# Squares of the values: single steps for the first batch, places of `v32` for its loads, and no gate for the later batches

## The chip, the cores and the metric

The kernel runs on one core of one Trainium2 chip. A core has TensorE (PE, matmuls; PEld is its weight load), VectorE (DVE), ScalarE (ACT), GpSimd (POOL) and SyncE (SP), which here issues all transfers of data. Each engine works through its own queue in order. The metric is device microseconds per execution, 941.67 us before the change (median of 3 runs, 940.76 to 941.94).

## The reference

Attention with a local window (32 positions for heads 0 to 3, every fourth of 128 positions for heads 4 to 7) over 8 batches of 576 positions and 8 heads of 64, and behind it a layer norm, an up-projection to 2048 with ReLU, a down-projection to 512, and a residual:

```python
scores = scale * np.matmul(q, k.transpose(0, 1, 3, 2))
scores = np.where(masks, scores, -1e9)          # masks: window, or dilated window
attn = softmax(scores)                          # with 1e-09 in the denominator
x = np.matmul(attn, v)                          # heads side by side: (B, S, 512)
xn = (x - mean) / np.sqrt(var + 1e-06) * g_ln
out = x + np.maximum(xn @ w_ch1, 0.0) @ w_ch2
```

The two weights come as float64, all else as float32.

## The kernel before, in words

**Tiles.** The 4608 rows are 36 tiles (`NT`) of 128, nine (`TPP`) to two batches of the reference; three tiles (`NB`) make a block for the feed-forward part. A tile goes through these steps: L loads q, k and v; A splits them into pairs of float16; S computes the scores, M the softmax, V the product with the values, N the norm, T the transposes; U are its up-matmuls and D its down-matmuls, with the output at the end. From the third block on, U and D are taken together for a block (`b2.5` is the sixth step of block 2). Tiles 0 to 3 (`EARLY`) skip A and work on float32. The weights are converted by C (w1, loaded at L655) and W (w2, also L655), each load followed by an ACT operation (L659), three on DVE (L661, L662, L666) and matmuls (L673), and split into float16 pairs by s (w1) and P (w2) with ACT at L153 and DVE at L154. P0 needs the scale of all of w2. D needs P, and U needs s and T.

**The scale of the values.** A float16 split of v needs a power of two as a scale. `scale_v(t0, t1)` makes one for the tiles of a batch, of which there are four: tiles 3 to 8, 9 to 17, 18 to 26 and 27 to 35. For each tile it loads the values once more, 256 KB, into a place called `row` (L225), squares them on ACT with a sum over each row into a column of `v_sums` (L226), and then adds the columns on DVE (L228), adds over the partitions by a matmul on PE (L230), copies the result out (L232) and makes the scale with four small DVE operations (L132 to L142). The split of a tile's values (`prep_v`, in A) waits for that scale.

**Places.** A named place comes in a number of copies: `row` has two, shared by the masks (once, at the start), these loads, and the outputs y of the down-matmuls; `v32` has two, for the values of tiles from 3 on (L194, and L293 for tile 3); `v_sums` has one, so a batch can't square before the batch ahead of it has added its columns; `ps_v`, in PSUM, has one, shared by V of all tiles and by L230; `slot` has five, for weights being converted, early values, q and k of odd tiles, and the split halves.

**What sets the order.** All steps are registered by `unit(name, when, what, *after)` with a number `when`, made larger than that of each step it comes after; `MOVED` puts other numbers in place of some. The steps are then written out sorted by that number. The number is only an order: a scheduler takes the written program, with the earlier step as the more urgent, and for each engine picks, at each point of its own model of time, the most urgent instruction whose inputs and place are there. An instruction written late can so be placed ahead of one written early. The order that it settles on is fixed for the engines, which then wait on semaphores. `tc.issue_after(x)` adds the condition that what its block writes for the engine of `x` comes behind `x` in that engine's queue.

**Around the change.** The first batch's step is `v3`, at 66.0. A later batch is written by `scale_later(t)` at 2 behind the start of A of tile 5, 14 or 23, and its transfers are held in SP's queue behind the load of that tile's own values (`state["load", t]`). Tile 5's own load is in turn held behind the last weight load written before it (`after_weights`). For the second batch the number of the step is 112 + 2 = 114; the first outputs come after P7, over 124.2.

Of the kernel before, what the change touches and what calls it, by code (L numbers as in the profile page):

```python
# [10 lines left out]
F32 = mybir.dt.float32  # L11
I32 = mybir.dt.int32
AF = mybir.ActivationFunctionType
ALU = mybir.AluOpType
AX = mybir.AxisListType
PSUM = bass.MemoryType.PSUM

P = 128
H = 8
HP = 4  # L20
D = 64
DM = 512
# [7 lines left out]
TPP = 9  # L30
NB = 3
NQK = 2 * HP * P
NBLK = NT // NB
EARLY = 4
AHEAD = 64.3
GAP = 17.2
SOFTMAX, VALUES, READY = 0.9, 23.0, 21.7
LOAD = -12.6
PER_TILE = 21.7
CW, SLOTS = 2, 5  # L40
HG = 4
SUMS = 128
NW2 = 2
SIGN_BIT = -(2**31)
V_GROUPS = (EARLY - 1, TPP)

TIMES = {
    "C": (0.0, 12.0, 30.0, 40.0), "E": (2.0, 22.0, 50.0, 75.0), "W": (50.0, 3.2), "P": 104.0,
    "U": (42.0, 66.0, 84.0), "D": 106.0, "v": 70.0, "X": 84.0, "t": (88.0, 112.0),
}  # L50

MOVED = {
# [6 lines left out]
}  # L59
APART = 2  # L60

# [7 lines left out]
def attention_then_ffn(ctx: ExitStack, tc, qkv, masks, g, w1, w2, out):  # L69
    nc = tc.nc  # L70

    const = ctx.enter_context(tc.tile_pool(name="const", bufs=1))
    work = ctx.enter_context(tc.tile_pool(name="work", bufs=2))
# [53 lines left out]
    def pow2_of(bound, top, squared, name):  # L127

        at = 2.0**23
        e = (189 if squared else 253) + top  # L130
        k = work.tile([P, 2], I32, name="sc_k")
        nc.vector.tensor_scalar(  # L132
            k[:, 0:1], bound.bitcast(I32), scalar1=24 if squared else 23, scalar2=23,
            op0=ALU.logical_shift_right, op1=ALU.logical_shift_left,
        )
        nc.vector.tensor_scalar(
            k[:, 1:2], k[:, 0:1], scalar1=(e - 252) * at, scalar2=-1.0, op0=ALU.max, op1=ALU.mult
        )
        s = const.tile([P, 2], F32, name=name)
        si = s.bitcast(I32)  # L140
        nc.vector.tensor_scalar(si[:, 0:1], k[:, 1:2], scalar1=e * at, scalar2=None, op0=ALU.add)
        nc.vector.tensor_scalar(  # L142
            si[:, 1:2], k[:, 1:2], scalar1=-1.0, scalar2=(254 - e) * at, op0=ALU.mult, op1=ALU.add
        )
        return s
# [13 lines left out]
    state = {}  # L159
# [6 lines left out]
    def load_tile(t):  # L166
        with after_weights() if t < NB * 2 else nullcontext():
            load_tile_now(t)
# [28 lines left out]
    def load_ranges(t, v32):  # L197
# [17 lines left out]
                        )  # L215
        return x

    def scale_v(t0, t1):

        if t0 % TPP == 0 or t0 == EARLY - 1:  # L220
            state["v_sums"] = work.tile([P, TPP], F32, name="v_sums", bufs=1)
        sums = state["v_sums"]
        for t in range(t0, t1):
            vs = work.tile([P, DM], F32, name="row")
            nc.sync.dma_start(out=vs, in_=qkv[t, :, NQK:])  # L225
            nc.scalar.activation(vs, vs, AF.Square, accum_out=sums[:, t % TPP : t % TPP + 1])  # L226
        tot = work.tile([P, 1], F32, name="v_tot")
        nc.vector.reduce_sum(tot, sums[:, t0 % TPP : (t1 - 1) % TPP + 1], axis=AX.X)  # L228
        ps = ps_v.tile([P, 2, 512], F32, name="ps_v")[:, 0]
        nc.tensor.matmul(ps[:, 0:1], ones.broadcast_to([P, P]), tot, start=True, stop=True)  # L230
        ss = work.tile([P, 1], F32, name="v_ss")
        nc.vector.tensor_copy(ss, ps[:, 0:1])  # L232
        sv = pow2_of(ss, T_V, True, f"sv{t0}")
        for t in range(t0, t1):
            state["sv", t] = sv

    def scale_later(t):
        with tc.issue_after(state["load", t]):
            t0 = (t // TPP + 1) * TPP
            scale_v(t0, t0 + TPP)  # L240

    def stack_v(t):

# [500 lines left out]
    def unit(name, when, what, *after):  # L744

        when = MOVED.get(name, when)
        for a in after:
            if a in units:
                when = max(when, units[a][0] + 0.001)
        units[name] = (when, len(units), what)  # L750
        return when
# [4 lines left out]
    at, pace = TIMES["W"]  # L756
    for f in range(0, NFC, CW):
        unit(f"W{f}", at + pace * f / CW, lambda f=f: load_w2(f), f"W{f - CW}", f"s{f // 4}")
    for n in range(NFC // NW2):
        unit(f"P{n}", TIMES["P"] + 0.01 * n, lambda n=n: split_w2(n), f"W{NFC - CW}", f"P{n - 1}")  # L760
    for a, b in zip(V_GROUPS, V_GROUPS[1:]):
        unit(f"v{a}", TIMES["v"], lambda a=a, b=b: scale_v(a, b), f"V{a - 1}")

    start = TIMES["D"] + 10.4 * NB
    t_at = 0.0
    for b in range(NBLK):
        blk = dict(t0=b * NB, b=b)
        for i in range(NB):
            t = b * NB + i
            if t < EARLY:  # L770
                t_at = TIMES["E"][t]
                if t:
                    unit(f"L{t}", t_at - 8.0, lambda t=t: load_tile(t), f"V{t - 2}")
                else:
                    unit("L0", 0.5, load_first)
                for n, (name, what) in enumerate((
                    ("S", scores_early), ("M", softmax_early), ("V", values_early), ("N", norm),
                )):
                    unit(f"{name}{t}", t_at + 3.0 * n, lambda t=t, what=what: what(t), f"L{t}", f"{name}{t - 1}")
                unit(  # L780
                    f"T{t}", t_at + 10.0, lambda t=t, i=i, blk=blk: transposes(t, blk, i), f"N{t}",
                    f"P{NFC // NW2 - 1}" if b else None,
                )
                if t == EARLY - 1:
                    unit(f"A{t}", TIMES["X"], lambda t=t: split_last(t), f"v{t}", f"N{t}")
                continue
            if t - EARLY < len(TIMES["t"]):
                t_at = TIMES["t"][t - EARLY]
            else:
                t_at = max(t_at + GAP, start - AHEAD - PER_TILE * (NB - 1 - i))  # L790

            def do(name, when, what, *after):
                return unit(f"{name}{t}", t_at + when, lambda t=t: what(t), f"{name}{t - 1}", *after)

            unit(f"L{t}", units[f"A{t - 1}"][0] + LOAD, lambda t=t: load_tile(t), f"A{t - 2}")


            t_at = do("A", 0, attn_prep, f"L{t}", f"V{t - 2}")
            if t % TPP == 5 and t + 4 < NT:
                do("v", 2, scale_later, f"A{t}")  # L800
            do("S", 6, attn_scores, f"A{t}")
            do("M", SOFTMAX, attn_softmax, f"S{t}", f"V{t - 1}")
            do("V", VALUES, attn_values, f"M{t}")
            do("N", VALUES + 2, norm, f"V{t}")
            unit(
                f"T{t}", t_at + READY, lambda t=t, i=i, blk=blk: transposes(t, blk, i),
                f"N{t}", f"P{NFC // NW2 - 1}" if b else None, f"b{b - 2}",
            )
        ups, downs = ffn(blk, b < APART)
        if b < APART:  # L810
            for i in range(NB):
                t = b * NB + i
                when = TIMES["U"][t] if t < len(TIMES["U"]) else start
                for fq in range(NKC):
                    us = ups[(4 * i + fq) * 4 // HG : (4 * i + fq + 1) * 4 // HG]
                    when = unit(
                        f"U{t}.{fq}", when, lambda us=us: [what() for _, what in us],
                        f"T{t}", f"s{fq}", f"U{t}.{fq - 1}", f"U{t - 1}.{fq}", f"D{t - 1 - i}.{fq}",
                    )
                    when += sum(took for took, _ in us)  # L820
                if b == 0:
                    when = TIMES["D"] + 10.4 * i
                for p in range(NKC):
                    took, what = downs[4 * i + p]
                    when = unit(
                        f"D{t}.{p}", when, what,
                        f"P{(4 * p + 3) // NW2}", f"U{t}.{p}", f"D{t}.{p - 1}", f"D{t - 2}.3" if p == 0 else None,
                    )
                    when += took
                start = max(start, when) if b else start  # L830
            last = tuple(f"D{t}.{NKC - 1}" for t in range((b + 1) * NB))
            units[f"b{b}"] = (max(units[a][0] for a in last), len(units), lambda: None)
        else:
            when = max(start, units[f"T{b * NB + NB - 1}"][0] + 0.1, max(units[a][0] for a in last))
            for n, (took, what) in enumerate(ups + downs):
                name = f"b{b}" if n == len(ups) + len(downs) - 1 else f"b{b}.{n}"
                when = unit(name, when, what, f"T{b * NB + NB - 1}", f"b{b}.{n - 1}", *last) + took
            last = (f"b{b}",)
            start = max(start + PER_TILE * NB, when)
    for _, _, what in sorted(units.values(), key=lambda e: e[:2]):  # L840
# [72 lines left out]
```

## Time and profile before

| | |
|---|---|
| median of three runs | 941.67 us |
| profiled execution | 944.02 us |
| span of its instructions | 942.2 us |
| PE busy | 890.7 us, 95% |
| DVE busy | 634.2 us, 67% |
| ACT busy | 312.7 us, 33% |
| POOL busy | 312.3 us, 33% |
| loads of values for squares | 33 of 256 KB, first at 19.2 us, last at 543.6 us |
| squares on ACT | 33, first at 27.0 us, last at 546.5 us |
| mean granted PE clock | 0.985 |

Times in the views are microseconds from the start of the span. A row of the order of time gives the start, the length, the engine, the source line, the operation with the places it writes and reads, and in brackets how long its engine was idle before it and what ended that. PE is near full from about 140 us to the end; before that the weights are loaded and converted while the first tiles are worked on.

### The profile page before, as it was taken

The page shows a single profiled execution, that of the slowest core. Times are in us where ns is not written, and L with a number is a line of the kernel's source. Part 1 is how long each engine was busy: PE and PEld are TensorE (multiplying, and loading weights), DVE is VectorE, ACT ScalarE, POOL GpSimd, SP SyncE. Part 2 cuts the span into 40 slices and gives each one's busy share as a digit, 9 for nine tenths or more (in the row PEclk, how much of TensorE's full clock was granted, in tenths as well). Part 3 has the DMA queues.
Part 4 walks back from the last instruction along what each step waited for, and adds up shares of the span by engine and source line. Part 5 has one row for each costly group of instructions (what it writes and reads, how often), then busy time and mean ns, then how long its engine had stood idle before and what let it go on. Part 6 is the DMA issues. An engine that isn't in the chain of part 4 may idle for free.

```text
span 942.2 us, 18610 instructions
## 1 busy us (share of the span) xinstructions
PE 890.7 (95%) x7608; PEld 552.2 (59%) x7608; DVE 634.2 (67%) x1379; ACT 312.7 (33%) x588; POOL 312.3 (33%) x319
## 2 busy tenths in 40 slices
PE   4479789999999999999999999999999999999998
PEld 4379466777665555565565565565565565564553
DVE  4799658896977577786686686686686685660210
ACT  4556742334323343251241451241241341130110
POOL 1010273646234235454253353354243341120000
PEclk9979899999999999999999999999999999999999
DMA  7887872754344516446143654364043411010000
GB/s 241 311 229 229 187 176 50 153 122 115 66 75 93 148 52 133 92 71 136 37 80 71 169 105 71 89 123 90 30 88 69 87 27 37 21 24 23 12 1 34
DMA packets 79622, 93.39 MB, mean 99 GB/s; under 512 B 47920, under 2 KB 53680, under 8 KB 79536
## 3 DMA queue, kind: packets, MB, share of 16 engines
q1 hardware_dynamic: 79536, 92.21, 42.3%
q8 instruction: 59, 0.97, 0.4%
q14 instruction: 27, 0.22, 0.1%
HBM read 71.86 MB, written 9.44 MB: 86 GB/s over the span
## 4 chain that ended last, share of the span: by engine, by line
PE 81%; DMA 10%; ACT 3%; DVE 3%; issue 2%; SPq 1%; POOL 1%; ACTq 0%; DVEq 0%; POOLq 0%
PE ps_f L597 36%; PE ps_f L620 35%; PE ps_s L330 4%; PE ps_v L528 4%; DMA row<-in_qkv 4%; DMA slot<-in_w 3%; DMA xT<-xl 1%; ACT row L226 1%; DMA slot<-in_qkv 1%; DMA v<-in_qkv 0%; PE ps_f L673 0%; ACT w_sb L153 0%; DVE slot L662 0%; POOL slot L280 0%; DVE slot L154 0%
## 5 line engine op out<-in xcount | busy, mean ns | idle before, releaser
L620 PE MATMUL ps_f<-w_sb,hh 128*128 128x512 f16 x1152 | 345.0, 380 | 5.8 <-ACT w_sb L153 5.0
L597 PEld LDWEIGHTS <-w_sb 128*128 128x128 f16 x3072 | 256.0, 99 | 126.6 <-issue 4.6
L620 PE MATMUL ps_f<-w_sb,hl 128*128 128x512 f16 x576 | 219.1, 380 | 0.0
L597 PE MATMUL ps_f<-xT,w_sb 128*128 128x384 f16 (+1 forms) x1536 | 199.2, 289 | 2.9 <-DMA xT<-xh 2.4
L597 PE MATMUL ps_f<-w_sb 128*128 128x384 f16 (+1 forms) x1536 | 196.7, 287 | 0.0
L620 PEld LDWEIGHTS <-hh 128*128 128x128 f16 x1152 | 111.8, 98 | 131.5 <-issue 6.8
L603 ACT ACTIVATE hh<-ps_f 128x384 f16<-128x384 f32 (+1 forms) x184 | 91.1, 500 | 216.8 <-PE ps_f L597 216.8
L604 DVE SCALAR_TENSOR_TENSOR hl<-ps_f,hh 128x384 f16<-128x384 f32 (+1 forms) x184 | 100.2, 569 | 42.4 <-ACT hh L603 40.3
L620 PEld LDWEIGHTS <-hl 128*128 128x128 f16 x576 | 56.5, 98 | 67.1 <-issue 1.8
L362 DVE TENSOR_TENSOR sc<-ps_s,mask 32x256 f32<-32x256 f32 x128 | 53.6, 419 | 51.2 <-PE ps_s L330 49.8
L435 DVE STREAM_TRANSPOSE pt_d<-pk 32x256 f32<-32x256 f32 x128 | 79.4, 621 | 1.8
L626 DVE SCALAR_TENSOR_TENSOR row<-ps_f,s,x 128x512 f32<-128x512 f32 x36 | 27.0, 749 | 74.5 <-PE ps_f L620 74.0
L446 POOL TENSOR_TENSOR sc<-sc,mx 128x512 f32<-128x512 f32 x32 | 33.4, 1043 | 116.3 <-DVE mx L444 116.3
L451 ACT ACTIVATE p<-sc 128x512 f32<-128x512 f32 x32 | 20.2, 631 | 128.2 <-POOL sc L446 128.2
L569 POOL TENSOR_TENSOR xl<-xn,xh 128x512 f16<-128x512 f32 x36 | 42.0, 1166 | 59.1 <-ACT xh L568 49.8
L330 PE MATMUL ps_s<-slot 128*128 128x128 f16 (+1 forms) x768 | 58.8, 226 | 2.1 <-DVE sc L348 2.1
L330 PEld LDWEIGHTS <-slot 128*128 128x128 f16 x768 | 50.9, 99 | 12.7 <-DVE sc L348 3.0
L287 POOL COPY slot<-slot 128x128 f16<-128x128 f16 x56 | 17.5, 340 | 119.4 <-PE ps_v L528 119.3
L348 DVE TENSOR_TENSOR sc<-ps_s,mask 32x256 f32<-32x256 f32 x128 | 53.5, 418 | 4.9 <-PE ps_s L330 3.4
L453 POOL TENSOR_TENSOR pk<-p,pk 128x512 f16<-128x512 f32 x32 | 40.7, 1271 | 45.8 <-ACT pk L452 45.8
L458 DVE STREAM_TRANSPOSE pt_b<-pk 32x128 f16<-32x128 f16 x87 | 26.1, 300 | 42.0 <-ACT pk L452 28.4
L554 POOL TENSOR_TENSOR rstd<-rstd,mhalf 128x1 f32<-128x1 f32 x36 | 21.1, 587 | 94.9 <-DVE rstd L553 85.2
(100 smaller groups left out, 961.3 us busy)
## 6 DMA issues: line engine op xcount, KB each, us to landing
qk<-in_qkv SPq DMA_DIRECT2D x36, 512.0 KB, 6.9
slot<-in_qkv SPq DMA_DIRECT2D x32, 512.0 KB, 6.7
slot<-in_w SPq DMA_DIRECT2D x14, 1024.0 KB, 6.3
out_x<-row SPq DMA_DIRECT2D x36, 256.0 KB, 2.0
row<-in_qkv SPq DMA_DIRECT2D x33, 256.0 KB, 2.9
v<-in_qkv SPq DMA_DIRECT2D x33, 256.0 KB, 3.0
slot<-in_w SPq DMA_DIRECT2D x4, 512.0 KB, 7.3
slot<-in_qkv SPq DMA_DIRECT2D x28, 64.0 KB, 4.5
```

What stands on the lines that cost most here:

```text
L330: nc.tensor.matmul(out, lhs, rhs, start=(n == 0), stop=(n == len(terms) - 1))
L348: nc.vector.tensor_tensor(out=sc[pj, 0:HP, :], in0=ps[pj, :, W * j : W * j + 2 * W], in1=mask_16[pj, m : m + 1, :].broadcast_to([W, HP, 2 ...
L362: nc.vector.tensor_tensor(out=sc[pj, HP:H, :].rearrange("p h (t i) -> p h t i", t=2), in0=ps[pj].rearrange("p h (t c) -> p h t c", t=2)[:, ...
L435: nc.vector.transpose(dd[pj].rearrange("p t h (i r) -> p r t h i", r=DIL)[:, j], pk[pj, HP:H, :].rearrange("p h (t i) -> p t h i", t=2),)
L446: nc.gpsimd.tensor_tensor(out=sm, in0=sc, in1=mx.broadcast_to([P, H, 2 * W]), op=ALU.subtract)
L453: nc.gpsimd.tensor_tensor(out=pk16[:, :, :, 1], in0=p32, in1=pk16[:, :, :, 0], op=ALU.subtract)
L528: nc.tensor.matmul(oo, l, r, start=(n == 0), stop=(n == len(mm) - 1))
L569: nc.gpsimd.tensor_tensor(out=xl, in0=xn, in1=xh, op=ALU.subtract)
L597: nc.tensor.matmul(z[:, n], l, r, start=(m == 0), stop=(m == len(mm) - 1))
L603: nc.scalar.activation(hh, z, AF.Relu)
L604: nc.vector.scalar_tensor_tensor(out=hl, in0=z, scalar=0.0, in1=hh, op0=ALU.max, op1=ALU.subtract)
L620: nc.tensor.matmul(o, l, r, start=(f == 0 and m == 0), stop=(f == NFC - 1 and m == 2))
```

## The change

The first batch's step is taken apart. Each of its six tiles gets a load step `y3` to `y8` and a square step `z3` to `z8`: loads at 33, 38, 43, 48, 53 and 58, the square 6 behind its load; the rest (`v3`: sum, matmul, scale) follows at 33 + 5 × 6 + 6 = 69, and `v3` has left `MOVED`. The loads go to places of `v32`. The later batches stay one step each with loads in `row`, but the step now stands 10 (`LATER`) behind the start of A and not 2, after A of its tile and after `v3`, and the condition that held its transfers behind a load is gone.

```diff
+SQUARE = 6.0
+LATER = 10.0
...
-    "U": (42.0, 66.0, 84.0), "D": 106.0, "v": 70.0, "X": 84.0, "t": (88.0, 112.0),
+    "U": (42.0, 66.0, 84.0), "D": 106.0, "v": (33.0, 5.0), "X": 84.0, "t": (88.0, 112.0),
...
-    "W6": 65.8, "b2.5": 240.4, "b2.6": 228.4, "v3": 66.0,
+    "W6": 65.8, "b2.5": 240.4, "b2.6": 228.4,
...
+    def load_values(t, name):
+        state["vs", t] = work.tile([P, H, D], F32, name="v32") if name == "v32" else work.tile([P, DM], F32, name="row")
+        x = state["vs", t]
+        x = x.rearrange("p h d -> p (h d)") if name == "v32" else x
+        nc.sync.dma_start(out=x, in_=qkv[t, :, NQK:])
+        state["vs", t] = x
+
+    def square_values(t):
+        if t % TPP == 0 or t == EARLY - 1:
+            state["v_sums"] = work.tile([P, TPP], F32, name="v_sums", bufs=1)
+        vs = state.pop(("vs", t))
+        nc.scalar.activation(vs, vs, AF.Square, accum_out=state["v_sums"][:, t % TPP : t % TPP + 1])
+
     def scale_v(t0, t1):
 
-        if t0 % TPP == 0 or t0 == EARLY - 1:
-            state["v_sums"] = work.tile([P, TPP], F32, name="v_sums", bufs=1)
-        sums = state["v_sums"]
-        for t in range(t0, t1):
-            vs = work.tile([P, DM], F32, name="row")
-            nc.sync.dma_start(out=vs, in_=qkv[t, :, NQK:])
-            nc.scalar.activation(vs, vs, AF.Square, accum_out=sums[:, t % TPP : t % TPP + 1])
         tot = work.tile([P, 1], F32, name="v_tot")
-        nc.vector.reduce_sum(tot, sums[:, t0 % TPP : (t1 - 1) % TPP + 1], axis=AX.X)
+        nc.vector.reduce_sum(tot, state["v_sums"][:, t0 % TPP : (t1 - 1) % TPP + 1], axis=AX.X)
...
-    def scale_later(t):
-        with tc.issue_after(state["load", t]):
-            t0 = (t // TPP + 1) * TPP
-            scale_v(t0, t0 + TPP)
...
-    for a, b in zip(V_GROUPS, V_GROUPS[1:]):
-        unit(f"v{a}", TIMES["v"], lambda a=a, b=b: scale_v(a, b), f"V{a - 1}")
+    def unit_v(a, b, at, pace, name):
+
+        for t in range(a, b):
+            when = at + pace * (t - a)
+            unit(f"y{t}", when, lambda t=t: load_values(t, name), f"y{t - 1}")
+            unit(f"z{t}", when + SQUARE, lambda t=t: square_values(t), f"y{t}", f"z{t - 1}", f"v{a - TPP}", f"v{EARLY - 1}" if a == TPP else None)
+        unit(f"v{a}", at + pace * (b - a) + SQUARE, lambda: scale_v(a, b), f"z{b - 1}")
+
+    unit_v(EARLY - 1, TPP, TIMES["v"][0], TIMES["v"][1], "v32")
...
             if t % TPP == 5 and t + 4 < NT:
-                do("v", 2, scale_later, f"A{t}")
+                def later(t):
+                    for n in range(t + 4, t + 4 + TPP):
+                        load_values(n, "row")
+                        square_values(n)
+                    scale_v(t + 4, t + 4 + TPP)
+
+                unit(f"v{t + 4}", t_at + LATER, lambda t=t: later(t), f"A{t}", f"v{EARLY - 1}")
```

More of the change, by code (lines that the diff above doesn't have):

```diff
@@ L44 @@
 SIGN_BIT = -(2**31)
-V_GROUPS = (EARLY - 1, TPP)
 TIMES = {
     "C": (0.0, 12.0, 30.0, 40.0), "E": (2.0, 22.0, 50.0, 75.0), "W": (50.0, 3.2), "P": 104.0,
-    "U": (42.0, 66.0, 84.0), "D": 106.0, "v": 70.0, "X": 84.0, "t": (88.0, 112.0),
+    "U": (42.0, 66.0, 84.0), "D": 106.0, "v": (33.0, 5.0), "X": 84.0, "t": (88.0, 112.0),
 }
```

## The prediction

> **What bounds the kernel now.** I read the busy times first, then the windows, to see where TensorE (PE) isn't full.
>
> ```profile
> PE 890.7 (95%) x7608; PEld 552.2 (59%) x7608; DVE 634.2 (67%) x1379; ACT 312.7 (33%) x588; POOL 312.3 (33%) x319
> ```
> ```profile
> 20.00:40.00 20.00, 9.30 (x159) 8.06 (x159) 14.08 (x23) 9.00 (x16) 0.12 (x1) 1.00 0.97 360
> 40.00:60.00 20.00, 11.76 (x110) 10.54 (x110) 17.84 (x34) 14.19 (x31) 3.51 (x3) 0.77 0.90 240
> 60.00:80.00 20.00, 19.23 (x345) 18.48 (x344) 19.99 (x35) 10.46 (x14) 2.16 (x2) 0.89 0.87 225
> 80.00:100.00 20.00, 18.84 (x382) 18.17 (x380) 17.68 (x39) 12.90 (x31) 1.71 (x2) 1.00 0.53 190
> 100.00:120.00 20.00, 15.39 (x66) 7.09 (x66) 10.88 (x11) 16.19 (x34) 7.23 (x5) 0.83 0.94 201
> 120.00:140.00 20.00, 15.39 (x208) 13.00 (x206) 10.01 (x27) 10.11 (x22) 13.40 (x15) 0.91 0.72 168
> 320.00:340.00 20.00, 17.41 (x113) 10.37 (x112) 8.49 (x24) 9.93 (x26) 2.31 (x2) 0.93 0.40 119
> 500.00:560.00 60.00, 60.00 (x459) 34.90 (x458) 44.15 (x105) 23.65 (x50) 21.76 (x23) 1.00 0.50 112
> ```
>
> Each window lists its length, then the busy us of PE, weight loads, DVE, ACT and POOL, then PE's granted clock, the DMA share and GB/s. PE is idle 942.2 − 890.7 = 51.5 us, 30.1 of them in 20:140, and 2.59 in 320:340. Around the third batch of squares (500:560) it is full. Up to 140 us the limit changes: 20:40 is DMA (share 0.97), 60:80 is DVE (19.99 of 20), 100:120 is ACT (16.19) and DMA (0.94). So the change is worth what it does before 140 us, and a little in 320:340.
>
> Next, SyncE's queue (start, length, transfer):
>
> ```profile
> 17.69 1.51 SPq L655 DMA_DIRECT2D slot<-in_w  x2
> 19.24 1.17 SPq L225 DMA_DIRECT2D row<-in_qkv  x2
> 20.57 0.43 SPq L655 DMA_DIRECT2D slot<-in_w  x1
> 27.71 0.94 SPq L225 DMA_DIRECT2D row<-in_qkv  x2
> 28.74 0.90 SPq L655 DMA_DIRECT2D slot<-in_w  x2
> 31.62 1.71 SPq L225 DMA_DIRECT2D row<-in_qkv  x2
> 95.91 0.73 SPq L194 DMA_DIRECT2D v<-in_qkv  x1
> 96.70 0.89 SPq L225 DMA_DIRECT2D row<-in_qkv  x2
> 123.44 0.33 SPq L225 DMA_DIRECT2D row<-in_qkv  x1
> 242.80 0.36 SPq L634 DMA_DIRECT2D out_x<-row  x1
> 261.46 0.58 SPq L194 DMA_DIRECT2D v<-in_qkv  x1
> 289.94 0.55 SPq L634 DMA_DIRECT2D out_x<-row  x1
> 313.21 0.66 SPq L225 DMA_DIRECT2D row<-in_qkv  x1
> ```
>
> Two things are to be seen. First, the written order doesn't hold a transfer back when its place is free: the first batch's six loads stand at 66.0 (`MOVED["v3"]`), behind W4 at 48.5, yet leave from 19.24. The nine loads of the second batch leave right behind the load of tile 5's values (95.91 to 96.70): their gate held them. Second, places of one name go in written order: between the output at 242.80 and the one at 289.94 no load of the third batch took a `row`, though its gate, the load of tile 14, had passed at 261.46, by count of the values' loads.
>
> **The change part by part.** *No work is added.* 33 loads of 256 KB, 33 squares and four sums stay. A square has this price, with 0.187 for reading the sum:
>
> ```profile
> L226 ACT ACTIVATE row<-row x33: 615/630/693, 27.0 to 546.5; 128x512 f32<-128x512 f32 x33
> SPq L225 <- ACT row L226: 15.7, 10, 6.6
> ```
>
> So only times move. The second line is SyncE before 140 us: 15 loads, 15.7 us of it waiting for a square to give back a place, 1.05 us a load.
>
> *Batch 0 (tiles 3 to 8): two places in `v32` in place of two in `row`, each load and square a step of its own at 33 to 64.* As deep as before; `v32` isn't wanted until tile 4's load, after 80 us. The loads already ran at 19 to 33, ahead of the new positions, so I cost it at 0. The bounds: SyncE stands still from 21.00 to 27.71 behind the third load, 6.7 us; if the weights (28.74) now pass it, up to 6.7 us come back, and if the earlier positions put a load ahead of a weight's, 256 KB at the 360 GB/s of 20:40 is 0.73 us each, 4.4 us for six. This batch's sum and scale move from 66 to 69, off the path: 0.
>
> *Batch 1 (tiles 9 to 17): the gate goes, and both `row` places are empty but for the masks.* This is what matters. By the queue's first lesson the loads leave as soon as SyncE has nothing better, from about 21 us. The first two squares wait for `v_sums` until batch 0's sum has read it (45.75 below), the other seven loads for a square each. So 9 × 256 KB and 9 × 0.82 us of ACT (630 + 187 ns, 7.4 us in all) go from 96 to 131 into 21 to 96. What they did where they were:
>
> ```profile
> 45.75 0.15 DVE L228 TENSOR_REDUCE v_tot<-v_sums 128x1 f32<-128x6 f32 x1
> 98.64 0.58 DVE L727 TENSOR_SCALAR s<-s,s 128x1 f32<-128x1 f32 x4
> 98.96 0.72 ACT L153 ACTIVATE vh<-v,sv 128x512 f16<-128x512 f32 x1 [3.63 <-DMA v<-in_qkv]
> 99.59 0.63 ACT L226 ACTIVATE row<-row 128x512 f32<-128x512 f32 x1
> 102.06 0.63 ACT L226 ACTIVATE row<-row 128x512 f32<-128x512 f32 x1 [1.74 <-DMA row<-in_qkv]
> 102.69 2.17 ACT L153 ACTIVATE w_sb<-w_sb,s 128x1024 f16<-128x1024 f32 x2
> 103.87 0.59 PE L620 MATMUL ps_f<-w_sb,hh 128*128 128x512 f16 x1 [5.04 <-ACT w_sb L153]
> 123.36 2.61 PE L476 MATMUL ps_v<-slot,pt_d 64*128 64x65 f32 x32
> 131.10 0.16 DVE L228 TENSOR_REDUCE v_tot<-v_sums 128x1 f32<-128x9 f32 x1 [4.37 <-ACT row L226]
> 131.61 0.76 DVE L486 TENSOR_TENSOR x<-ps_v,rs 128x256 f32<-128x256 f32 x2
> 132.51 0.54 PE L230 MATMUL ps_v<-v_tot,ones 128*128 128x1 f32 x2 [4.61 <-DVE x L486]
> ```
>
> (a) PE waits 5.04 us for the first split of w2. Its scale is ready at 99.22 (98.64 + 0.58), and ACT is behind the vh at about 99.6, but two squares, the second waiting for its load, hold the split until 102.69. Without them it starts 3.1 us sooner: **−3.1**. The vh's wait for `v` stays, so not all 5.04 come back.
>
> (b) From 126.7 DVE stands behind the sum of batch 1, which waits 4.37 us for the last square (loaded at 123.44). Behind it in DVE's order is tile 3's x, whose PSUM place PE's L230 waits for, with all of PE's work behind it: 4.61 us. With the squares done early, x follows its matmuls (over at 126.0) at once: **−4.6**. What is late next is the ordinary queue of up-matmuls behind L230; PE is full from 132.5.
>
> (c) What the loads cost where they go. Two in 20:40 at 360 GB/s take 2 × 0.262 MB / 360 = 1.5 us from the weights. DMA idles there only 3%, so I count it whole. The seven gated ones: DMA's idle shares in 40 to 96 come to 2.0 + 2.6 + 7.5 = 12.1 us (0.10, 0.13 of 20 and 0.47 of 16), and 1.84 MB at 360 GB/s want 5.1 us. So bandwidth is there, but each can hold SyncE for 1.05 us with a weight load or a transpose behind it: 7 × 1.05 = 7.4 us. DVE, the limit in 60:80, has weights queued up, so I take a little over a quarter of that, 2.0. Together **+3.5**. Bounds: 0 (all in gaps) and 1.5 + 5.1 + 7.4 = 14.0 us (nothing hidden).
>
> On this the Trainium skill speaks against the change: "DMA: Bandwidth & Descriptors", section on the anatomy of one DMA, says that a semaphore wait is held at the issuing sequencer, ahead of dispatch, so that a transfer that waits for a square stops everything behind it. The trace agrees, with SyncE silent from 21.00 to 27.71; by it alone the 7.4 us would count whole and the sum would come to +1.2, which is rival B at work, with its price below.
>
> (d) The granted clock after both PE gaps:
>
> ```profile
> 103.87:109.00 5.13, 4.39 (x11) 1.51 (x11) 4.43 (x5) 5.13 (x9) 0.53 (x1) 0.53 0.95 232
> 132.50:137.00 4.50, 4.49 (x49) 4.33 (x50) 4.16 (x15) 0.55 (x2) 4.42 (x4) 0.62 0.06 15
> ```
>
> 5.13 × 0.47 = 2.4 us and 4.50 × 0.38 = 1.7 us are lost to it. A gap elsewhere would bring it back, so the sum takes 0 and the range up to −4.1. "TensorE: Matmul & The Clock Gate", Part 1, in the Trainium skill, gives a window of about 3.4 us of idling before the clock halves; by it the shortened first gap (5.04 − 3.1 = 1.9 us) and the closed second one would keep it, and the sum would be −8.3 us, which still lies in the forecast's own range. The trace shows only that gaps of 5.04 and 4.61 us drop it.
>
> *Batches 2 and 3: gate gone, ten instead of two behind the tile's start.* Their loads wait for the outputs ahead of them in the ring of `row`, not for the gate. I take 0; bounds −2.6 (the idle in 320:340) and +2.6 (as much again).
>
> **Sum**: −3.1 − 4.6 + 3.5 = −4.2 us. The profiled execution took 944.02 us, its span 942.2 and 1.8 around it; that would be 939.8. Against the median of three runs, 941.67, it is 937.5.
>
> **The rivals.** *B, the weights starve (slower).* Place: SyncE's and ACT's queues from 45 to 96, where the gap-filling loads and squares stand ahead of weights. Its price is (c) at its upper end, 14.0, less the 7.7 of (a) and (b): +6.3, about 948. It decides once the split of w2 is put off by over 7.7 us. For it: SyncE's 15.7 us of such waits, DVE full in 60:80. Against: the 12.1 us of DMA idling, and ACT idle 5.8 to 9.5 us in each window from 40 to 100.
>
> *C, the second batch doesn't move.* If SyncE or DVE's sum of batch 0 has no gap before the weights are through, the loads leave near 96 as before, and the sum with its stall at 131 stays: 941.7. For it: they now stand at 122, behind more work. Against: batch 0 went 47 units ahead of its position.
>
> *D, batch 0 helps too.* Its squares as early steps let weights pass SyncE's 6.7 us of standing: −10.9 us in all, about 931. For it, what the weights' conversion on ACT waited for, and the last weight's load:
>
> ```profile
> 38.79 1.12 ACT L659 ACTIVATE w_sb<-slot 128x1024 f32<-128x1024 f32 x1 [6.59 <-DMA slot<-in_w]
> L655 SPq DMA_DIRECT2D slot<-in_w x18: 368/390/942, 2.1 to 82.7; - x18
> ```
>
> The load of 28.74 came 6.59 us late for ACT. Against: two places as before, so the third load still needs a square.
>
> **How the numbers follow.** The forecast 0.42, B 0.33, C 0.15, D 0.10. The forecast's own range is 933 to 940. With (d) and 320:340 below D and (c) above, 930 to 949 holds the time 8 times in 10. A measurement tells 0.2%, 1.9 us, from no change: faster 0.42 + 0.10 = 0.52, same 0.15, slower 0.33.
>
> **What would show it.** Right: L225's loads of nine leave between 20 and 96, batch 1's last square ends before 96, the 4.37 and 4.61 us waits are gone, and PE's first down-matmul starts near 104.3 or sooner (103.87 − 3.1 + 3.5). Wrong: nine loads still behind 95.91 (C); or weight loads (L655) ending well after 82.7 us, where the last one issued, and the first down-matmul past 108 (B); or weights issued at 24 rather than 28.74 (D). An idle stretch of PE that grows after 140 us would be outside all of these.

## The result, and the profile after

The changed kernel takes 953.51 us (median of 4 runs, 950.83 to 955.03), against 941.81 us for the kernel before on the same chip: ratio 1.0119, interval 1.0090 to 1.0148, so slower by 11 us. The prediction said 937.5 us and faster.

The profiled execution's span is 952.4 us, up from 942.2 us. The page's busy times of the changed kernel:

```profile
PE 891.0 (94%) x7608; PEld 552.0 (58%) x7608; DVE 636.9 (67%) x1379; ACT 311.6 (33%) x588; POOL 313.0 (33%) x319
```

PE has the same work (890.7 before); its idle time grew from 51.5 to 61.4 us. The windows of the changed kernel (columns as in the prediction) say where:

```profile
40.00:60.00 20.00, 15.04 (x145) 14.08 (x146) 16.80 (x26) 15.09 (x32) 1.40 (x2) 0.66 0.87 269
60.00:80.00 20.00, 13.88 (x257) 12.57 (x255) 15.57 (x32) 10.30 (x19) 0.55 (x1) 0.76 0.87 276
80.00:100.00 20.00, 14.97 (x226) 14.01 (x224) 18.13 (x25) 12.84 (x32) 2.83 (x3) 0.98 0.49 164
100.00:120.00 20.00, 19.92 (x300) 14.06 (x305) 12.78 (x28) 13.80 (x28) 4.71 (x4) 1.00 0.65 142
120.00:140.00 20.00, 13.68 (x148) 9.43 (x142) 12.31 (x21) 9.26 (x15) 17.39 (x16) 0.91 0.65 146
340.00:360.00 20.00, 15.17 (x126) 9.28 (x125) 13.57 (x37) 8.60 (x20) 5.13 (x7) 1.00 0.55 93
```

And one window of the kernel before that the prediction doesn't show:

```profile
340.00:360.00 20.00, 20.00 (x195) 12.72 (x194) 17.38 (x44) 8.65 (x15) 11.67 (x12) 0.98 0.41 84
```

In 60:100 PE lost 9.2 us (28.85 busy, 38.07 before); 4.5 of that came back in 100:120, where 115 up-matmuls ran (none before), and 3.3 had been gained in 40:60 (15.04 busy). Then 120:140 lost 1.7, and the third batch's place, 340:360, lost 4.8. DVE, which was full in 60:80, had nothing to do for 4.4 us there: ACT, which converts the weights ahead of it, waited 7.5 us in this window for their loads (3.9 before), and DVE 3.4 for one of the conversions.

SyncE's queue of the changed kernel (start, length, transfer) shows that the second batch did move:

```profile
21.47 1.09 SPq L223 DMA_DIRECT2D row<-in_qkv  x2
...
63.66 1.56 SPq L223 DMA_DIRECT2D row<-in_qkv  x2
65.33 0.38 SPq L657 DMA_DIRECT2D slot<-in_w  x1
...
77.40 0.34 SPq L223 DMA_DIRECT2D row<-in_qkv  x1
...
87.33 0.38 SPq L657 DMA_DIRECT2D slot<-in_w  x1
```

Its nine loads leave from 21.47 to 77.40, and the last weight leaves at 87.33, not 82.7. The order of time in the changed kernel shows something that the prediction had not looked for:

```profile
92.46 2.61 PE L478 MATMUL ps_v<-slot,pt_d 64*128 64x65 f32 x32
98.84 0.35 PE L237 MATMUL ps_v<-v_tot,ones 128*128 128x1 f32 x2 [1.04 <-DVE x L488]
100.69 0.15 DVE L239 COPY v_ss<-ps_v 128x1 f32<-128x1 f32 x1
102.18 1.33 ACT L154 ACTIVATE vh<-v,sv 128x512 f16<-128x512 f32 x2
106.29 2.19 ACT L154 ACTIVATE w_sb<-w_sb,s 128x1024 f16<-128x1024 f32 x2 [2.30 <-DVE s L729]
107.77 0.59 PE L622 MATMUL ps_f<-w_sb,hh 128*128 128x512 f16 x2
```

The first batch's scale: its matmul L237 waits for tile 2's `x` and stands behind tile 2's product with the values (L478). In the kernel before it stood ahead of that product by 13 us:

```profile
77.46 0.30 PE L230 MATMUL ps_v<-v_tot,ones 128*128 128x1 f32 x2
90.52 2.61 PE L476 MATMUL ps_v<-slot,pt_d 64*128 64x65 f32 x32
91.01 0.71 ACT L153 ACTIVATE vh<-v,sv 128x512 f16<-128x512 f32 x1
```

So the first split of values (vh) went from 91.01 to 102.18 us.

### The profile page after: what moved, and what is told of

The parts are those of the page before. It is cut to its first block, busy times and chain, and to the rows that moved or that the text cites. A ratio compares the mean times of both kernels' runs of the same rounds, so it can differ in the third digit from the quotient of the medians.

```text
span 952.4 us, 18606 instructions
## 1 busy us (share of the span) xinstructions
PE 891.0 (94%) x7608; PEld 552.0 (58%) x7608; DVE 636.9 (67%) x1379; ACT 311.6 (33%) x588; POOL 313.0 (33%) x319
## 4 chain that ended last, share of the span: by engine, by line
PE 76%; DMA 4%; DVE 3%; POOL 3%; ACT 2%; issue 1%; SPq 1%; ACTq 0%; POOLq 0%; DVEq 0%
PE ps_f L622 35%; PE ps_f L599 33%; PE ps_s L332 4%; PE ps_v L530 4%; DMA qk<-in_qkv 1%; DMA row<-in_qkv 1%; POOL slot L282 1%; DVE pt_d L437 1%; POOL slot L311 1%; DMA xT<-xl 1%; DMA v<-in_qkv 1%; SPq L187 0%; POOL sc L448 0%; DVE pt_a L434 0%; DVE sc L364 0%
```

## The experiments

The change was taken apart into four: the single steps with `v32`, the place of `v3` in the written order (66 or 69), the gate, and the position of the later batches (2 or 10). These are most of their combinations; the time of each is a median, its ratio is to the kernel before on the same chip.

| kernel | steps, `v32` | `v3` | gate | position | us | ratio, 95% interval |
|---|---|---|---|---|---|---|
| before | no | 66 | yes | 2 | 941.81 | 1 |
| e6 | yes | 66 | yes | 2 | 942.53 | 1.0003 [0.9980, 1.0027] |
| e7 | no | 69 | yes | 2 | 951.77 | 1.0100 [1.0050, 1.0150] |
| e4 | yes | 69 | yes | 2 | 951.87 | 1.0100 [1.0066, 1.0134] |
| e8 | yes | 66 | yes | 10 | 946.06 | 1.0043 [1.0028, 1.0059] |
| e1 | yes | 69 | yes | 10 | 957.41 | 1.0159 [1.0128, 1.0190] |
| e20 | no | 66 | no | 2 | 940.21 | 0.9973 [0.9957, 0.9990] |
| e3 | no | 66 | no | 10 | 945.94 | 1.0053 [1.0038, 1.0069] |
| e11 | yes | 66 | no | 2 | 949.14 | 1.0067 [1.0044, 1.0090] |
| e2 | yes | 69 | no | 2 | 948.07 | 1.0058 [1.0034, 1.0081] |
| e5 | yes | 66 | no | 10 | 951.58 | 1.0089 [1.0059, 1.0119] |
| after | yes | 69 | no | 10 | 953.51 | 1.0119 [1.0090, 1.0148] |

**e1, the gate put back, and e2, position 2.** Each against the changed kernel:

```diff
-                    for n in range(t + 4, t + 4 + TPP):
...
+                    with tc.issue_after(state["load", t]):
+                        for n in range(t + 4, t + 4 + TPP):
...
```


> The changed kernel with the gate put back: the loads of each later batch again stand in SyncE's queue behind the load of their tile's values; position still 10, batch 0 still as single steps in v32. Theory 1 (the gate's absence is what costs at the start, because batch 1's loads and squares go among the weights; the position of 10 costs at the third batch): no load in row between 20 and 95 us, PE idle before 140 us back at about 42 us from 45.5, the third batch's loss of some 5 us stays, so about 946 to 948. Theory 2 (batch 0's single steps cost): stays at about 953. Theory 3 (the position alone costs): about 950 to 953.

```diff
-LATER = 10.0
+LATER = 2.0
```


> The changed kernel with the later batches' step 2 behind the tile's start in place of 10; no gate, batch 0 as single steps in v32. Theory 1: the start as in the changed kernel (nine loads of row between 21 and 78 us, PE idle before 140 us near 45), the third batch as before the change (PE idle in 320:360 about 2.6 us in place of 7.8), so about 948. Theory 2: about 953. Theory 3: about 942.

With the gate back the time didn't fall but rose, by 4 us, to 957.41, which none of the three theories had. So in the changed kernel as it stands the early loads of the second batch are a gain rather than a loss; the later runs show why. Position 2 brought 5 us (948.07), as theory 1 had it.

**e3, the gate off in the kernel before, and e4, the steps alone.** e3 is the kernel before with the gate taken away and position 10. e4 is the changed kernel with the gate and position 2, that is, with the edits of e1 and e2 together:

```diff
-        with tc.issue_after(state["load", t]):
-            t0 = (t // TPP + 1) * TPP
-            scale_v(t0, t0 + TPP)
+        t0 = (t // TPP + 1) * TPP
+        scale_v(t0, t0 + TPP)
...
-                do("v", 2, scale_later, f"A{t}")
+                do("v", 10, scale_later, f"A{t}")
```


> The kernel of before with the gate taken off and the later batches' step at 10, batch 0 as one step with loads in row as before. Theory 1: batch 1's loads go between batch 0's last and 96 us, one place at a time among the weights, and the time is that of the changed kernel, 950 to 955. Theory 2: about 942. Theory 3: about 950 to 953.

```diff
-LATER = 10.0
+LATER = 2.0
...
+                    with tc.issue_after(state["load", t]):
...
```


> Batch 0's single steps with places of v32 alone: the gate is back and the later batches' step stands at 2 as before. Theory 1: within 2 us of 941.8, since the loads of batch 0 leave as before, from about 19 us. Theory 2: about 953. Theory 3: 941.8.

e3 costs 4 to 5 us, less than theories 1 and 3 had and more than theory 2; e8 and e20 below say of what. e4 went against what was expected: the first batch's part alone, priced at nothing, costs 9.4 us (1.0100 of 942). e4 in the order of time:

```profile
88.79 2.61 PE L478 MATMUL ps_v<-slot,pt_d 64*128 64x65 f32 x32
93.93 0.35 PE L237 MATMUL ps_v<-v_tot,ones 128*128 128x1 f32 x2
95.84 0.15 DVE L239 COPY v_ss<-ps_v 128x1 f32<-128x1 f32 x1
97.41 1.41 SPq L249 DMA_DIRECT2D v_b<-vh  x2
107.32 1.07 SPq L195 DMA_DIRECT2D v<-in_qkv  x2
108.44 0.93 SPq L223 DMA_DIRECT2D row<-in_qkv  x2
136.32 0.33 SPq L223 DMA_DIRECT2D row<-in_qkv  x1
142.93 0.63 ACT L230 ACTIVATE row<-row 128x512 f32<-128x512 f32 x1 [5.52 <-DMA row<-in_qkv]
143.91 0.59 PE L237 MATMUL ps_v<-v_tot,ones 128*128 128x1 f32 x2 [5.30 <-DVE v_tot L235]
```

Again the scale comes behind tile 2's values (L478), and the copy L239 comes at 95.84. SyncE's queue carries the delay on: it stands 15.6 us, until 97.41, at the transfer of the split values (L249), which waits for the split. In the kernel before it stood there 7.0 us:

```profile
91.75 3.16 SPq L247 DMA_DIRECT2D v_b<-vh  x4
```

Behind it in the queue come tile 5's values, at 107.32 (95.91 before), and the gated loads of the second batch, from 108.44 to 136.32 (96.70 to 123.44 before). The last square comes at 142.93 (130.35 before), and PE stands 5.30 us for the sum, at 143.91.

**e5, e6 and e7: is it the number of v3?** e5 is the changed kernel, e6 is e4, e7 is the kernel before, each with one edit:

```diff
-    "W6": 65.8, "b2.5": 240.4, "b2.6": 228.4,
+    "W6": 65.8, "b2.5": 240.4, "b2.6": 228.4, "v3": 66.0,
```


> The changed kernel with batch 0's sum, matmul and scale (v3) put back to 66.0, ahead of V2 at 68.2; loads, squares, places and the missing gate as changed. Theory 4 (the matmul of that scale takes the one place of ps_v in written order, and at 69 it stands behind V2, so that the scale comes 20 us later: copy of the sum at 100.7 us in place of 80.8): the copy is back near 81 us, the time falls by about as much as the single steps cost alone (10), to 943 to 947, which is what taking the gate off alone gave. Theory 2b (the loads' and squares' own early positions cost): stays at 951 to 955.

> Batch 0's single steps with places of v32, gate back, the later step at 2, and v3 back at 66.0, so that nothing but the loads and squares of batch 0 differs from before. Theory 4: within 2 us of before, 939 to 943 (the last weight load left 1.9 us sooner with the steps alone). Theory 2b: 950 to 952 as with the steps alone.

```diff
-    "W6": 65.8, "b2.5": 240.4, "b2.6": 228.4, "v3": 66.0,
+    "W6": 65.8, "b2.5": 240.4, "b2.6": 228.4, "v3": 69.0,
```


> The kernel of before with one number changed: v3 at 69.0 in place of 66.0, behind V2. All six loads and squares of batch 0 stay in that step. Theory 4: the copy of the sum moves from 80.8 to 95 us or later, the time to 949 to 953. Theory 2b: within 2 us of before.

e6 and e7 settle it. Steps and `v32` without the move of `v3` cost nothing (1.0003; the scheduler gives every engine the order of the kernel before, and only the places of the six loads differ), and the move of `v3` alone costs what e4 costs (1.0100). Between 66 and 69 the list of steps holds two others, `V2` at 68.2 (tile 2's values) and `U1.1` at 68.6. With `v3` at 68.19 the scheduler writes PE's instructions in the order of the kernel before, but for the scale's matmul, which stands one matmul later; at 68.3 it writes the order of e7. Neither was run. So it is the step across `V2`. `ps_v` has one place, and V of each tile and the scale's matmul take it in written order, even where the later one could run first.

e5 says that in the changed kernel this counts for little, against what was expected (943 to 947): 951.58 against 953.51, with overlapping intervals. The late scale does its harm through the gated loads of the second batch, and there they are no longer gated. SyncE stands in the changed kernel too, 13.7 us until 102.30, for the late split; but by then all nine loads have left (the last at 77.40).

**e9, e10, e16: the scale's matmul in another PSUM place.** If the place of `ps_v` is the cause, another place should cure it. e9 is the changed kernel, e10 the kernel before, e16 is e10 with `v3` at 69:

```diff
-        ps = ps_v.tile([P, 2, 512], F32, name="ps_v")[:, 0]
+        ps = ps_f.tile([P, 512], F32, name="ps_f")
```


> The changed kernel with the scale's small matmul in a place of ps_f (four of them) in place of the one of ps_v; v3 stays at 69. Theory 4: the scale of batch 0 no longer waits for tile 2's values, the copy of its sum comes before 90 us, and the time falls by several us, to 942 to 948; a place of ps_f held by it may cost an up-matmul a wait of 1 to 2 us. Theory 2b: stays at 951 to 955.

> The kernel before with one edit: the scale's matmul (L230) takes a place of ps_f, which the up- and down-matmuls use in turn, and no longer the one place of ps_v. Theory (the place of ps_v, taken in written order, is what the late scale paid for): ahead of V2 the place was free anyway, so 942, 938 to 946, by what the other order in ps_f costs. Rival (a place of ps_f is itself dear, as the 967.5 of the changed kernel with this edit suggests): 950 or more.

> The same with v3 at 69 and so behind V2 in the written order. Theory (place of ps_v): the matmul no longer waits for tile 2's values, the copy L232 stays before 90 us against 95.5 in ps_v, and the time stays within 3 us of the run with v3 at 66 in ps_f. Rival (a later scale costs by its lateness, whatever its place): 9 us above that run. Third: a place of ps_f is dear, both near 950 or more.

None came out as the theory had it: e9 967.47 us (ratio 1.0261 [1.0217, 1.0306]), e10 983.76 (1.0447 [1.0422, 1.0472]), e16 991.66 (1.0525 [1.0495, 1.0556]). The window of e10 around the third batch's scale shows where it loses:

```profile
320.00:360.00 40.00, 23.17 (x221) 17.03 (x220) 35.34 (x86) 16.74 (x36) 17.96 (x18) 0.70 0.60 136
```

PE is busy 23.17 us of 40, against 37.41 in the kernel before and 36.62 in e17 below, where only the first scale is in `ps_f`. So the later batches' scales in `ps_f` are what costs. That the up- and down-matmuls then wait behind them, because the places of `ps_f` too go in written order, is argued; no run shows it. e16 spoke for the rival: its first scale runs at 83.99, ahead of tile 2's values (88.49), and the move of `v3` still costs 7.9 us (991.66 − 983.76).

**e17, e18, e19: only the first batch's scale in ps_f.** e17 is the kernel before with this, e18 the same with `v3` at 69, e19 the changed kernel with it:

```diff
-        ps = ps_v.tile([P, 2, 512], F32, name="ps_v")[:, 0]
+        ps = ps_f.tile([P, 512], F32, name="ps_f") if t0 == EARLY - 1 else ps_v.tile([P, 2, 512], F32, name="ps_v")[:, 0]
```


> The kernel before with the matmul of the first batch's scale alone in a place of ps_f; the three later ones stay in ps_v. Theory (the 983.8 of the run before came from the later batches' scales, behind which up-matmuls wait for a place of ps_f; PE's 23.17 us busy of 40 in 320:360 say so): 942, 939 to 945, and 320:360 back near 37.4 us busy. Rival (the first batch's place in ps_f is dear too): 950 or more, idle before 140 us.

> The same with v3 at 69, behind V2. Theory (the place of ps_v in written order is what cost 9.4 us): the first scale's matmul now stands ahead of tile 2's values on PE, the copy L232 comes before 88 us rather than at 95.5, and the time is within 3 us of the run with v3 at 66 in ps_f. Rival (lateness of the number itself, whatever the place): 7 to 10 us above it.

> The changed kernel with the first batch's scale alone in ps_f. Theory: the late scale's part goes, the missing gate (6 us) and the position 10 of the third batch (4 us) stay: 951, 948 to 954, as with v3 at 66, and the copy L239 before 90 us against 100.7. Rival (the late scale was the whole of the 11.7 us): 944 or less.

e17: 941.46 us, 0.9988 [0.9965, 1.0012]. e18: 944.58, 1.0028 [1.0006, 1.0051]. So with another place the move of `v3` costs 3.1 us (944.58 − 941.46, just at what the intervals can tell apart), where in `ps_v` it cost 9.4. e18 in the order of time:

```profile
83.17 0.33 PE L230 MATMUL ps_f<-v_tot,ones 128*128 128x1 f32 x2
83.54 0.16 DVE L232 COPY v_ss<-ps_f 128x1 f32<-128x1 f32 x1 [0.31 <-PE ps_f L230]
87.67 2.61 PE L476 MATMUL ps_v<-slot,pt_d 64*128 64x65 f32 x32
90.41 1.34 ACT L153 ACTIVATE vh<-v,sv 128x512 f16<-128x512 f32 x2
```

With the same late number the scale's matmul is again ahead of tile 2's values, the copy at 83.54 rather than 95.46 in e7, and the split at 90.41; the second batch's loads start at 97.08 rather than 107.84. By these two runs about 6 of the 9.4 us are the place and the rest goes with the later number. The 7.9 us between e10 and e16, where the place was `ps_f` as well, don't fit that, so how the 9.4 us divide stays open. e19 took 953.03 us (1.0135 [1.0095, 1.0175]): as in e5, curing the late scale doesn't help the changed kernel.

**e8 and e11: what else the changed kernel has.** e8 is e1 (steps, gate, position 10) and e11 is e2 (steps, no gate, position 2), both with this:

```diff
-    "W6": 65.8, "b2.5": 240.4, "b2.6": 228.4,
+    "W6": 65.8, "b2.5": 240.4, "b2.6": 228.4, "v3": 66.0,
```


> The changed kernel with the gate back and v3 back at 66.0, so that against before only batch 0's single steps and the position of 10 remain. Theory 4 with the position as a second cause (10 in place of 2 pushes the later batches' loads behind more work and its sum ends later): 2 to 6 us over before, in 320:360 or 120:160. If the position only costs behind a late scale: within 2 us of before.

> The changed kernel with v3 back at 66.0 and the later step at 2, so that against before only batch 0's single steps and the missing gate remain. If the missing gate costs by itself (the prediction's rival B, weights behind squares): 3 to 9 us over before, PE idle in 60:80 near 7 us in place of 0.8. If the missing gate gains, as it did behind a late scale (4 us): 2 to 4 us under before.

*Position 10* costs 4 us (e8 against e6, 1.0043 to 1.0003) and 5.7 in the changed kernel (against e2, 1.0119 to 1.0058); the other pairs of the table give 2.1 (e5 against e11), 5.6 (e1 against e4) and 7.5 (e3 against e20). The changed kernel at its third batch, in order of time:

```profile
336.10 1.40 PE L332 MATMUL ps_s<-slot 128*128 128x128 f16 x16 [2.96 <-DVE sc L350]
340.44 0.54 SPq L223 DMA_DIRECT2D row<-in_qkv  x1
347.54 0.63 ACT L230 ACTIVATE row<-row 128x512 f32<-128x512 f32 x1 [5.52 <-DMA row<-in_qkv]
348.30 0.16 DVE L235 TENSOR_REDUCE v_tot<-v_sums 128x1 f32<-128x9 f32 x1 [4.74 <-ACT row L230]
348.52 0.38 PE L237 MATMUL ps_v<-v_tot,ones 128*128 128x1 f32 x2 [3.34 <-DVE v_tot L235]
```

and e2, with position 2:

```profile
326.51 10.99 SPq L223 DMA_DIRECT2D row<-in_qkv  x7
340.92 0.38 PE L237 MATMUL ps_v<-v_tot,ones 128*128 128x1 f32 x2 [2.42 <-DVE v_tot L235]
```

At position 2 the last seven loads of the batch go one behind the other, from 326.51 to 337.50. At position 10 the step is written later, other transfers come between, and the ninth load leaves at 340.44; ACT, DVE and PE each stand waiting for it. PE waits for the sum in both, 3.34 us against 2.42. The rest of the loss is two more waits of PE: for the scores of the next tile (336.10) 2.96 us against 0.70, and for the copy of the sum 1.49 us, which e2 doesn't have. Together PE is idle 7.8 us in 320:360 against 3.1.

*The missing gate with v32* costs 6.3 us (e11, 1.0067). e11 in order of time:

```profile
64.60 1.84 SPq L223 DMA_DIRECT2D row<-in_qkv  x2
66.55 0.38 SPq L657 DMA_DIRECT2D slot<-in_w  x1
69.15 1.00 SPq L223 DMA_DIRECT2D row<-in_qkv  x2
74.39 1.12 ACT L661 ACTIVATE w_sb<-slot 128x1024 f32<-128x1024 f32 x1 [4.11 <-DMA slot<-in_w]
76.18 0.39 PE L599 MATMUL ps_f<-xT,w_sb 128*128 128x128 f16 x2 [5.40 <-ACT w_sb L154]
107.98 2.19 ACT L154 ACTIVATE w_sb<-w_sb,s 128x1024 f16<-128x1024 f32 x2 [1.44 <-DVE s L729]
109.18 0.59 PE L622 MATMUL ps_f<-w_sb,hh 128*128 128x512 f16 x2 [1.31 <-ACT w_sb L154]
130.91 0.35 PE L237 MATMUL ps_v<-v_tot,ones 128*128 128x1 f32 x2 [1.46 <-DVE x L488]
```

Pairs of `row` loads at 64.60 and 69.15 stand between the weights. ACT waits 4.11 us for a weight and PE 5.40 for the split made of it. This is what rival B said would happen. The place shows in every trace: PE is idle 0.7 to 1.7 us in 60:80 in the twelve kernels with the gate, 6.1 to 7.2 in the six without it and with `v32`, 4.0 and 4.1 in e20 and e3. The first split of w2 comes at 107.98, 5.3 us later than the 102.69 of before, but that says less: e5 has the same order of transfers up to 90 us, and there it comes at 101.28. So a time of a few us between two executions can't be read off their rows alone. The stall at 131 shrank, from 4.61 to 1.46 us.

**e20, the gate off and nothing else.** e3 had shown 93.25 us of PE busy in 20:140, 3.3 more than before, although its gate is off, and lost 3.8 in 320:360, where position 10 costs. So the gate was taken from the kernel before, at position 2, with all loads in `row`; the edit is the first half of e3's.

> The kernel before with the gate of the later batches taken away and nothing else: loads of all batches in row, one step a batch, position 2, v3 at 66. Theory (the missing gate only hurts together with v32, because with the loads in row the first batch's six loads keep both places and the second batch comes singly between the weights; the run with position 10 had 93.25 us of PE busy in 20:140 against 89.9, and lost it again in 320:360): 939, 937 to 941.5, with about 93 us busy in 20:140 and 37 in 320:360, last weight load before 85 us. Rival (a missing gate costs 6 us whatever the place of the loads): 946 to 950, with the first w2 split near 108.

940.21 us, 0.9973 [0.9957, 0.9990]: faster than both kernels. e20's window, and then its order of time:

```profile
20.00:140.00 120.00, 92.94 (x1327) 77.62 (x1326) 98.09 (x175) 73.96 (x147) 32.03 (x28) 0.94 0.82 232
```
```profile
46.32 0.38 SPq L225 DMA_DIRECT2D row<-in_qkv  x1
46.80 0.39 SPq L654 DMA_DIRECT2D slot<-in_w  x1
...
80.50 4.06 SPq L654 DMA_DIRECT2D slot<-in_w  x2
105.68 1.01 PE L619 MATMUL ps_f<-w_sb,hh 128*128 128x512 f16 x2 [3.08 <-ACT w_sb L153]
130.58 0.33 PE L230 MATMUL ps_v<-v_tot,ones 128*128 128x1 f32 x2
```

The first batch's six loads keep both places of `row` until their last squares, at 42.07 and 42.68, so the second batch can't start at 21; it starts at 46.32, and most of its loads go singly. No weight load starts after 84.56 us (80.50 + 4.06). The first down-matmul is 1.8 us later than before, and the wait of 4.61 us before the second scale's matmul is gone altogether.

**e12 and e13: all later batches as single steps.** Both have `v3` at 66 and the gate. In e12 the loads and squares of all later batches are steps of their own, 4.5 apart, each square 6 behind its load; in e13 only those of the third and fourth, 6 apart:

```diff
...
-                unit(f"v{t + 4}", t_at + LATER, lambda t=t: later(t), f"A{t}", f"v{EARLY - 1}")
+                        when = t_at + LATER + PACE * (n - t - 4)
+                        unit(f"y{n}", when, lambda n=n, t=t: load_gated(n, t), f"A{t}", f"v{EARLY - 1}", f"y{n - 1}")
+                        unit(f"z{n}", when + SQUARE, lambda n=n: square_values(n), f"y{n}", f"z{n - 1}")
+                    unit(f"v{t + 4}", t_at + LATER + PACE * TPP + SQUARE, lambda t=t: scale_v(t + 4, t + 4 + TPP), f"z{t + 3 + TPP}")
...
```


> An attempt to beat both: batch 0 as changed with v3 at 66.0, and each later batch's loads and squares as single steps too, 4.5 apart from 2 behind the tile's start, gate kept, loads in row. If stalls of ACT and DVE on loads that come late are what the squares cost (5.0, 4.6 and 2.6 us of PE idle before), spreading them takes most of that away: 934 to 940. If the spread only moves the stalls: 940 to 945.

> As the one before, but batch 1 stays one step at 2 behind the tile's start and only batches 2 and 3 are spread, 6 apart. The start stays as before; the 2.6 us of PE idle in 320:340 and its lower clock go: 938 to 941 against before's 942. If the spread only moves the stall: as before.

e12 missed: 952.05 us, 1.0104 [1.0086, 1.0121]. Its PE is busy 97.93 us in 20:140, 8.0 more than before, but loses 2.4 us in 140:160, 3.7 in 160:320 and 4.0 in 320:360. What holds it there stays open. e13 took 941.34, 0.9985 [0.9967, 1.0004], which can't be told from before.

## Why the prediction was wrong

By single edits the way from before to after goes 0.9973 (gate off, e20), 1.0067 (steps and `v32`, e11), 1.0058 (`v3` at 69, e2), 1.0119 (position 10): −2.5, +8.9, −0.8 and +5.7 us of 942. The other way round it is +0.3 (steps, e6), +9.1 (`v3`, e4), −4.0 (gate, e2), +5.7 (position 10). The parts are not independent. With the steps and `v32` in, the runs stand like this, in us over the kernel before, at position 2 and at position 10:

| | gate | no gate |
|---|---|---|
| `v3` at 66 | +0.3, +4.0 | +6.3, +8.4 |
| `v3` at 69 | +9.4, +15.0 | +5.5, +11.2 |

The late scale costs 9 us alone and the early loads 6, and both together no more than one of them. So in the changed kernel neither repair alone helps much (gate back +3.8, `v3` back −2.8, both with overlapping intervals), and both together bring it to e8, 7 us lower. The forecast of −4.2 was 15.4 us off: 9.7 us lie at position 2 (e2, +5.5), 5.7 in position 10. The steps of the prediction stand like this.

**"This batch's sum and scale move from 66 to 69, off the path: 0" is the step that failed by itself.** It is +9.4 us (e7). The prediction had the rule in hand ("places of one name go in written order", read from `row`) and had named the PSUM place for which L230 waits at 132.51; it did not put the two together for the first batch, where the move crosses `V2` at 68.2. In the changed kernel, though, this cost shows only little (e5, e19), because the missing gate takes away the path by which it works.

**(c), +3.5 within 0 to 14.0, was mis-sized.** With `v3` still at 66 the second batch's loads among the weights make +6.3 us (e11) where the sum said −4.2. "I take a little over a quarter of that" rested on DVE having weights queued up; in the changed kernel DVE ran dry for 4.4 us in 60:80. By the prediction's own sum, the gains of 7.7 and e11's +6.3 make (c) 14.0, its upper bound. But the gains didn't come whole. The stall at 131 shrank by 3.2 us and not 4.6, and of (a)'s 3.1 there is no sign: the first split of w2 is at 101.28 to 108.38 in the six traces without the gate and with `v32`, and at 96.77 to 103.79 in the seven with the gate and `v3` at 66. With only the 3.2 as a gain, (c) would be about 9.5, an estimate from e11. Rival B named the mechanism, the place and a price: about 948, and e11 has 949.14. That the price fits is partly luck, since it takes both gains as won and wanted the split over 7.7 us late (past 110.39), which no trace shows.

"DMA: Bandwidth & Descriptors" of the Trainium skill, section on the anatomy of one DMA, says that a semaphore wait is held at the issuing sequencer before dispatch. The traces agree: in e11 SyncE waits three times, 8.3 us in all, for squares to give back a `row`, and in e4 15.6 us for a split with the gated loads behind it. It pointed the right way: by it alone the prediction's sum was +1.2. What neither the Trainium skill nor the prediction saw is that the price hangs on the places: with the first batch's loads in `row`, the same missing gate is a gain (e20).

**"(Batch 0) I cost it at 0"** holds only with the gate (e6, 1.0003). Without it, the emptied places of `row` let the second batch go at 21 us, in pairs, and that is worth +8.9 us (e20 to e11). It is the places and not the single steps: with its six first loads in `v32`, and still in one step, e20's program comes out of the scheduler in the order of e11 on every engine, and e11's with these loads in `row` in the order of e20 (neither was run). The prediction saw the places empty ("this is what matters") and counted it as the gain. Rival D is out: in e6 no weight left early.

**"Batches 2 and 3: I take 0", bounds ±2.6**, failed too: position 10 costs 2.1 to 7.5 us in five pairs, 5.7 in the changed kernel, outside the bounds in all but one. Idle time in 320:340 was taken as a limit on the loss, but idle time limits only what can be gained; a wait can be longer than any that is there.

**(b), −4.6, was right in mechanism.** In e20 the wait before the second scale's matmul is gone; in the changed kernel the second batch's sum is done at 83.09 us; but 1.46 us of it is left in e11 and 2.94 in e2. (a) and (c) together: e20's down-matmul comes 1.8 us later where −3.1 + 3.5 = +0.4 was said. That −4.6 + 1.8 = −2.8 is near the 2.5 us that e20 gained is partly luck: the 1.8 is between two executions, and the sum leaves out the clock.

**(d), the clock**, 0 to −4.1, came by half in e20: behind the second sum, where the gap is gone, the granted clock is 1.00 in 130.50:135.00, and was 0.62 in 132.50:137.00 before (1.7 us). Behind the first split it is 0.50 in 105.68:110.80, as it was 0.53 in 103.87:109.00 before, behind a shorter gap (3.08 us).

Where the 11 us sit in the changed kernel: PE idle before 140 us grew by 3.1 (20 − 6.89 and 120 − 87.66, against 20 − 7.74 and 120 − 89.91), in 140:320 by 1.7, in 320:360 by 5.2, which together are the 9.9 us that its idle time grew in all. So 6.8 us lie after 140 us, which the prediction had called outside all its rivals.

## What to carry to other kernels

Before moving a step in a written order, list the steps it is moved past and ask of each whether it shares a named place with it: a place with one copy makes neighbours in the list wait for each other, even where no data passes between them, and a small number (66 to 69) can be dear. Two faults can hide each other, so take a change apart in pairs and not only one by one. A gate on early transfers is worth what stands in the queue that they would enter; here empty places went with more of them going in, so the two have to be judged together. A bound on a loss is not the idle time that is there now. And rows of two executions can be some us apart for the same order of work; a few us are told by medians.

## What was not expected of the hardware

In e20 the granted clock was 0.50 in 105.68:110.80 behind a PE wait of 3.08 us, ahead of which PE had been busy without a break (6.60 of 6.60 us in 96.00:102.60), and 0.50 in 78.75:83.00 behind a wait of 2.85 us (the ends of matmuls are modelled in the profile). The Trainium skill, "TensorE: Matmul & The Clock Gate", Part 1, gives an idle window of about 3.4 us. Both waits measured here are shorter, so here the measurement decides.

The 16 DMA engines moved 386 GB/s in the changed kernel's 20:40, 393 in e11's and 405 in e5's, at a DMA share of 1.01 to 1.03, where the kernel before had 360 at 0.97: the room that the prediction took as 3% was more like 7 to 13%.
